# Attention into a squared-ReLU FFN on one core: the first batch planned, the second batch's q and k turned on TensorE

## The chip, the cores and the metric

The kernel runs on one core of one Trainium2 chip. The metric is the device time of one execution in microseconds (us). The program is one instruction stream for each of the five engines (TensorE, VectorE, ScalarE, GpSimd, SyncE), tied together by semaphores.

## What is computed

Grouped-query attention, whose output is reshaped to rows of tokens and goes straight into a feed-forward layer with a squared ReLU. Inputs and output are f32; the kernel computes in bf16 with f32 sums.

```python
batch, n_q_heads, n_kv_heads, seq, head_dim = (8, 16, 4, 384, 64)
k = np.repeat(k, group, axis=1); v = np.repeat(v, group, axis=1)   # group = 4
scores = np.matmul(q, k.transpose(0, 1, 3, 2)) / np.sqrt(D)
attn = softmax(scores)                       # max subtracted, rows divided by their sum
x = np.matmul(attn, v).transpose(0, 2, 1, 3).reshape(B * S, H * D)   # 3072 x 1024
h = np.maximum(x @ w_in, 0.0)                # 1024 -> 2048
out = (h * h) @ w_out                        # 2048 -> 1024
```

## The kernel before

**Recorder and planner.** Every operation goes through `Recorder.add`, which keeps for each engine a list in program order, works out the semaphore waits from the names of what is read and written, and advances a clock of its own per engine by a `cost` written by hand. Nothing is reordered at run time: the order in which operations were added is the order in which each engine carries them out. DMAs with the same `dma` tag also wait for one another. The estimated clocks are used by the main loop (L516 on) as a planner: at each step it lists what TensorE could do next (a value block `av`, a score burst `sc`, a piece of FFN `ffn`), estimates with `R.when` when the operands and a PSUM bank will be free, and takes by priority the first that is ready, or else the earliest.

**Attention of a batch.** There are four key groups of four query heads and 384 positions, that is 12 units of 128 keys. Keys are copied twice side by side in bf16 (`dup_k`, L241), so that two heads share TensorE as two halves of 64 rows. Keys and queries must then be transposed (`kT`, `qT`). Score bursts write PSUM; ScalarE applies the exponential into `expT` (L319, L339); a value block (`av`, L354) multiplies by the values, which carry a column of ones for the row sums; VectorE divides (L361, L367) into `o_sb`, which is transposed to `xT`, the FFN's input. `expT` holds 8 units, `o_sb` 3 groups, `xT` 3 batches; the staging tiles `q_st`, `k_st`, `v_st` hold 2 batches.

**Batch 0** is written out by hand ahead of the planner. Each key group gets a VectorE copy of its keys, transposes on TensorE (`turn_k_pe` L269, `turn_q_pe` L284) with evictions by VectorE (L274, L290), and then 18 small score bursts in all with exponentials of 128x1024 (L309, L319); value blocks and output turns on TensorE (L385, L391) are put in at fixed places. These turns use PSUM banks 6 and 7, the small bursts banks 0 to 5.

**Batches 1 to 7** are planned. GpSimd copies keys and values, and the DMA transposes of SyncE turn keys, both halves of the queries, and the outputs (`turn_k_dma` L250, `turn_q_dma` L256, `turn_o_dma` L372); all share the tag `turn`, so one runs at a time. Score bursts take two units at once over banks 0 to 5, with exponentials of 128x3072 (L329, L339).

**FFN.** For each batch, 16 column blocks of w_in in two half pieces each (L409), ReLU by VectorE (L419), square by ScalarE (L421), then 6 output blocks of w_out in four pieces each (L437), eviction (L449) and store (L452), on banks 6 and 7. It is the planner's lowest priority, and so fills TensorE wherever attention has nothing ready.

**Loads.** All loads are issued by GpSimd, which casts f32 to bf16 on the way, into one queue in program order: k, q and v of batch 0, four chunks of w_in, k, q and v of batch 1, four more chunks, and w_out in four parts. Loads of a later batch are issued when the staging tiles of two batches earlier are planned free. A warm-up of 24 matmuls on zeros (L486) precedes the work of TensorE.

Of the kernel before, what the change touches and what calls it, by code (L numbers as in the profile page):

```python
# [133 lines left out]
def bass_gqa_attention__then__ffn_squared_relu_kernel(  # L134
# [31 lines left out]
    q_st = [sb(f"q_st{i}", [128, H, NJ * D]) for i in range(NST)]  # L166
    k_st = [sb(f"k_st{i}", [128, NU, D]) for i in range(NST)]
    k_dup = [sb(f"k_dup{i}", [128, NU, 2, D]) for i in range(2)]
    v_st = [sb(f"v_st{i}", [128, NU, D]) for i in range(NST)]
# [28 lines left out]
    def load_k(b):  # L198
# [38 lines left out]
    def dup_k(b, eng, g0=0, g1=HKV):  # L237
        n = (g1 - g0) * NJ
        src = k_st[b % NST][:, g0 * NJ:g1 * NJ, :].unsqueeze(2).to_broadcast([128, n, 2, D])
        dst = k_dup[b % 2][:, g0 * NJ:g1 * NJ, :, :]  # L240
        R.add(eng, lambda e: e.tensor_copy(dst, src), reads=[("k_st", b % NST)],  # L241
              writes=[("k_dup", b % 2, g) for g in range(g0, g1)],
              cost=(0.15 * n / 3 + 0.1) if eng == "vector" else 0.33 * n)
# [17 lines left out]

    def turn_k_pe(b, g):
        i = pick((6, 7))
        pt = bank(i).bitcast(bf16)

        def tr(pe):
            for j in range(NJ):
                src = k_dup[b % 2][:, g * NJ + j].rearrange("p x d -> p (x d)")
                m = pe.matmul(pt[:, j * 128:(j + 1) * 128], src, ident[:], is_transpose=True)  # L269
# [7 lines left out]
    def turn_q_pe(b, g):  # L277
        i = pick((6, 7))
        pt = bank(i).bitcast(bf16)
# [22 lines left out]
    def burst_small(b, pieces, base):  # L302
# [3 lines left out]
        def sc(pe):  # L306
            for n, (u, c0) in enumerate(pieces):
# [11 lines left out]
        R.add("scalar", lambda e: e.activation(dst, src, AF.Exp, scale=0.125),  # L319
              reads=keys, writes=[("expT", (n + m) % NEX, c0 // 512) for m in range(len(pieces))], cost=0.89)  # L320

    def burst_two(b, u):

        def sc(pe):
            for k0, cols in ((0, ((0, 512), (512, 768))), (1, ((0, 256), (256, 768)))):
# [13 lines left out]
        R.add("scalar", lambda e: e.activation(dst, src, AF.Exp, scale=0.125),  # L339
              reads=keys, writes=[("expT", (n + m) % NEX, h) for m in range(2) for h in range(2)], cost=2.4)  # L340

# [36 lines left out]
    def turn_o_pe(b, c):  # L378
        i = pick((6, 7))
        pt = bank(i).bitcast(bf16)  # L380
# [95 lines left out]
    load_w_out(0, 0)  # L476
    load_w_out(0, 1)
    load_w_out(1, 0)
    load_w_out(1, 1)

# [3 lines left out]
    def warm_up(pe):  # L484
        for _ in range(24):
            m = pe.matmul(bank(7)[:, 0:256], warm[:, 0:128], warm[:, :])  # L486
        return m

    R.add("tensor", warm_up, reads=["warm"], writes=[("bank", 7)], cost=5.0)
# [7 lines left out]
    begun = -1  # L497
    todo = []
    for n, pieces in enumerate(smalls):
        g = pieces[-1][0] // NJ  # L500
        if g > begun:
            begun = g
            dup_k(0, "vector", g, g + 1)
            turn_k_pe(0, g)
            turn_q_pe(0, g)
            if g == 0:
                aug_v(0, "vector")
        burst_small(0, pieces, 2 * (n % 3))
        if n in (5, 8, 14):
            g = (5, 8, 14).index(n)  # L510
            todo += [lambda c=2 * g + i: av(0, c, (6, 7)) for i in range(2)]
            todo += [lambda c=2 * g + i: turn_o_pe(0, c) for i in range(2)]
        if todo:
            todo.pop(0)()
    while todo:
        todo.pop(0)()  # L516
# [4 lines left out]
    units, pairs, turned, x_done, up_done = NU, 6, 0, -1, -1  # L521
    loaded, queued = 1, 0
    chores = []
# [9 lines left out]
    def feed():  # L533
        for b in range(B):
            for n, item in enumerate(ffn(b)):
                yield (b, n) + item

    feeding = feed()
    f_head = next(feeding)
    margin = 0.5  # L540
    while av_q or sc_q or f_head is not None:
        now = R.clock["tensor"]
        if loaded + 1 < B and turned >= loaded + 1 - NST:
            loaded += 1
            load_k(loaded)
            load_q(loaded, 0, 16)
            load_v(loaded)
# [3 lines left out]
        while chores and R.when(reads=chores[0][0], eng="none") <= now + margin:  # L551
            chores.pop(0)[1]()
            if not chores:
                turned = queued
        cand = []
        if av_q:
            b, c = av_q[0]
            banks = (6, 7) if b == 0 else tuple(range(6))
            if units >= b * NU + (c // 2 + 1) * NJ and up_done >= b - NXT:
                t = max(R.when(reads=av_reads(b, c // 2)), min(R.when(writes=[("bank", i)]) for i in banks))  # L560
                cand.append((t, 0, "av"))
        if sc_q:
            b, u = sc_q[0]
            if turned >= b and pairs // 2 * NJ + NEX >= b * NU + u + 2:
                t = max(R.when(reads=score_reads(b, u) + score_reads(b, u + 1)),
                        R.when(writes=[("bank", i) for i in range(6)]))
                cand.append((t, 1, "sc"))
        if f_head is not None:
            b, n, need, banks, piece = f_head
            if x_done >= b:  # L570
                t = R.when(reads=need)
                if banks:
                    t = max(t, min(R.when(writes=[("bank", i)]) for i in banks))
                cand.append((t, 2, "ffn"))
        if not cand:
# [5 lines left out]
        what = min(ready, key=lambda x: x[1]) if ready else min(cand)  # L581
        if what[2] == "av":
            b, c = av_q.pop(0)
            av(b, c, banks=(6, 7) if b == 0 else tuple(range(6)))
            pairs += 1
            if b == 0:
                turn_o_pe(b, c)
            elif c % 2 == 1:
                turn_o_dma(b, c // 2)
            if c == 7:  # L590
                x_done = b
        elif what[2] == "sc":
            b, u = sc_q.pop(0)
            burst_two(b, u)
            units += 2
        else:
# [34 lines left out]
```

## Time and profile before

| | |
|---|---|
| runs | 460.81, 461.68, 464.22 us (median 461.68) |
| profiled execution | 463.22 us, with a span of 460.8 us from its first to its last instruction |
| TensorE busy | 431.8 us, 94% |
| mean granted TensorE clock | 0.963 |
| ScalarE, VectorE, GpSimd busy | 194.6, 157.7, 49.9 us |
| moved by DMA | 44.67 MB, mean 97 GB/s |

The profile is of one execution. PE is the matmul part of TensorE, PEld its weight loads, DVE is VectorE, ACT ScalarE, POOL GpSimd, SP SyncE; POOLq and SPq are the queues from which DMAs are issued. A line such as L329 is a line of the kernel; `ps<-qT,kT` names what an instruction writes and reads. A granted clock of 0.50 is half speed. Matmul durations are modelled to their end, so successive ones overlap; the distance between weight loads is nearer to the rate.

### The profile page before, as it was taken

The page shows a single profiled execution, that of the slowest core. Times are in us where ns is not written, and L with a number is a line of the kernel's source. Part 1 is how long each engine was busy: PE and PEld are TensorE (multiplying, and loading weights), DVE is VectorE, ACT ScalarE, POOL GpSimd, SP SyncE. Part 2 cuts the span into 40 slices and gives each one's busy share as a digit, 9 for nine tenths or more (in the row PEclk, how much of TensorE's full clock was granted, in tenths as well). Part 3 has the DMA queues.
Part 4 walks back from the last instruction along what each step waited for, and adds up shares of the span by engine and source line. Part 5 has one row for each costly group of instructions (what it writes and reads, how often), then busy time and mean ns, then how long its engine had stood idle before and what let it go on. Part 6 is the DMA issues. An engine that isn't in the chain of part 4 may idle for free.

```text
span 460.8 us, 7732 instructions
## 1 busy us (share of the span) xinstructions
PE 431.8 (94%) x3412; PEld 235.0 (51%) x3412; DVE 157.7 (34%) x328; ACT 194.6 (42%) x189; POOL 49.9 (11%) x59
## 2 busy tenths in 40 slices
PE   7668099997999999999999999999999999999997
PEld 4434055444565455554565554565465456445543
DVE  2343034222452244442344423353243224213411
ACT  3661067404766447744577445724033014103300
POOL 8740004013040200201000000000000000000000
PEclk9777589998999999999999999999999999999999
DMA  9999999769698796944705432004200110020011
GB/s 107 194 195 192 197 182 174 99 134 204 91 130 96 145 192 104 120 78 93 177 18 80 100 87 63 1 19 81 85 24 1 68 68 1 23 86 30 2 60 76
DMA packets 99762, 44.67 MB, mean 97 GB/s; under 512 B 81296, under 2 KB 93584, under 8 KB 99728
## 3 DMA queue, kind: packets, MB, share of 16 engines
q0 software_dynamic: 37488, 17.83, 31.6%
q1 hardware_dynamic: 62240, 26.35, 27.1%
q8 instruction: 26, 0.43, 0.4%
q14 instruction: 8, 0.07, 0.0%
HBM read 35.65 MB, written 12.58 MB: 105 GB/s over the span
## 4 chain that ended last, share of the span: by engine, by line
PE 90%; DMA 6%; ACT 2%; POOL 1%; DVE 1%; issue 0%
PE ps L437 36%; PE ps L409 36%; PE ps L354 8%; PE ps L329 7%; DMA qT<-q_st 3%; DMA kT<-k_dup 2%; ACT expT L319 1%; PE ps L486 1%; PE ps L309 1%; ACT expT L339 1%; POOL k_dup L241 0%; PE ps L385 0%; POOL q_st L214 0%; DVE qT L290 0%; POOL k_st L200 0%
## 5 line engine op out<-in xcount | busy, mean ns | idle before, releaser
L409 PE MATMUL ps<-xT,w_in_sb 128*128 128x384 bf16 x1024 | 177.2, 331 | 0.0
L437 PE MATMUL ps<-w_out_sb,h2T 128*128 128x512 bf16 x768 | 172.4, 379 | 0.0
L339 ACT ACTIVATE expT<-ps 128x3072 bf16<-128x3072 f32 x42 | 114.5, 2726 | 88.9 <-PE ps L329 88.2
L409 PEld LDWEIGHTS ps<-xT,w_in_sb 128*128 128x128 bf16 x1024 | 98.9, 99 | 72.5 <-issue 9.9
L421 ACT ACTIVATE h2T<-hr 128x384 bf16<-128x384 f32 x128 | 64.6, 520 | 139.7 <-DVE hr L419 139.6
L437 PEld LDWEIGHTS ps<-w_out_sb,h2T 128*128 128x128 bf16 x768 | 72.7, 98 | 87.8 <-issue 5.7
L419 DVE TENSOR_SCALAR hr<-ps 128x384 f32<-128x384 f32 x128 | 71.3, 557 | 122.2 <-PE ps L409 122.2
L449 DVE COPY y_sb<-ps 128x512 f32<-128x512 f32 x48 | 33.2, 692 | 125.1 <-PE ps L437 125.1
L354 PE MATMUL ps<-v_aug,expT 128*128 128x65 bf16 x1152 | 45.0, 199 | 7.6 <-ACT expT L319 4.7
L354 PEld LDWEIGHTS ps<-v_aug,expT 128*128 128x128 bf16 x1152 | 42.7, 101 | 15.3 <-ACT expT L319 5.5
L329 PE MATMUL ps<-qT,kT 64*128 64x512 bf16 (+1 forms) x336 | 35.2, 330 | 10.7 <-DMA qT<-q_st 10.7
L367 DVE TENSOR_TENSOR o_sb<-ps,rinv 128x384 bf16<-128x384 f32 x64 | 35.7, 558 | 2.2
L329 PEld LDWEIGHTS ps<-qT,kT 64*128 64x128 bf16 x336 | 13.1, 95 | 31.8 <-DMA qT<-q_st 11.1
L361 DVE RECIPROCAL rinv<-ps 128x6 f32<-128x6 f32 x64 | 12.2, 191 | 40.0 <-PE ps L354 39.9
L214 POOL DMA_DIRECT2D q_st<-in_q_dram x11 | 11.1, 1016 | 121.0 <-DMA qT<-q_st 121.0
L319 ACT ACTIVATE expT<-ps 128x1024 bf16<-128x1024 f32 x18 | 17.5, 1028 | 14.1 <-PE ps L309 14.1
L246 POOL COPY v_aug<-v_st 128x768 bf16<-128x768 bf16 x7 | 5.8, 831 | 64.8 <-PE ps L354 63.3
L309 PE MATMUL ps<-qT,kT 64*128 64x512 bf16 (+1 forms) x48 | 7.6, 387 | 3.3 <-DVE qT L290 2.6
L241 POOL COPY k_dup<-k_st 128x1536 bf16<-128x1536 bf16 x7 | 10.4, 1480 | 0.0
L224 POOL DMA_DIRECT2D w_in_sb<-in_moe_w_in_dram x8 | 7.1, 957 | 0.0
L200 POOL DMA_DIRECT2D k_st<-in_k_dram x8 | 6.2, 770 | 6.9 <-DVE k_dup L241 6.1
L486 PE MATMUL ps<-warm 128*128 128x256 bf16 x24 | 5.3, 416 | 1.1 <-DVE v_aug L482 1.1
(24 smaller groups left out, 37.8 us busy)
## 6 DMA issues: line engine op xcount, KB each, us to landing
out_dram<-y_sb SPq DMA_DIRECT2D x48, 256.0 KB, 2.0
q_st<-in_q_dram POOLq DMA_DIRECT2D x7, 768.0 KB, 11.5
w_in_sb<-in_moe_w_in_dram POOLq DMA_DIRECT2D x8, 512.0 KB, 17.0
w_out_sb<-in_moe_w_out_dram POOLq DMA_DIRECT2D x4, 1024.0 KB, 40.6
k_st<-in_k_dram POOLq DMA_DIRECT2D x8, 192.0 KB, 9.6
v_st<-in_v_dram POOLq DMA_DIRECT2D x8, 192.0 KB, 11.8
q_st<-in_q_dram POOLq DMA_DIRECT2D x4, 192.0 KB, 5.6
xT<-o_sb SPq DMA_TRANSPOSE x28, 2.9
```

What stands on the lines that cost most here:

```text
L309: m = pe.matmul(ps[:, base + x, n * wide:(n + 1) * wide], kT[b % 2][64 * x:64 * x + 64, u, :], q_cols(b, u // NJ, x, c0, c0 + wide))
L319: R.add("scalar", lambda e: e.activation(dst, src, AF.Exp, scale=0.125), reads=keys, writes=[("expT", (n + m) % NEX, c0 // 512) for m in r ...
L329: m = pe.matmul(flat[:, k0 * HC + c0:k0 * HC + c1], kT[b % 2][64 * x:64 * x + 64, u + k0, :], q_cols(b, (u + k0) // NJ, x, c0, c1))
L339: R.add("scalar", lambda e: e.activation(dst, src, AF.Exp, scale=0.125), reads=keys, writes=[("expT", (n + m) % NEX, h) for m in range(2) ...
L354: m = pe.matmul(po[:, f - 6 * s2, 0:D + 1], w, v_aug[b % 2][:, g * NJ + j, 0:D + 1], start=(j == 0), stop=(j == NJ - 1))
L361: R.add("vector", lambda e: e.reciprocal(rinv[r].ap().unsqueeze(2), po[:, :, D:D + 1]), reads=[("bank", i)], writes=[("rinv", r)], cost=0.13)
L367: R.add("vector", lambda e: e.tensor_tensor(dst, srcv, rbv, ALU.mult), reads=[("bank", i), ("rinv", r)], writes=[("o_sb", o, s2)], cost=0.48)
L409: m = pe.matmul(bank(i)[:, 0:S], w_in_sb[:, kc, c * 128:(c + 1) * 128], xT[b % NXT][:, kc, :], start=(kc == 0), stop=(kc == NKC - 1))
L419: R.add("vector", lambda e: e.tensor_scalar_max(hr[r][:, :], bank(i)[:, 0:S], 0.0), reads=[("bank", i)], writes=[("hr", r)], cost=0.48)
L421: R.add("scalar", lambda e: e.activation(h2T[b % 2][:, c, :], hr[r][:, :], AF.Square), reads=[("hr", r)], writes=[("h2T", b % 2, c)], cost ...
L437: m = pe.matmul(bank(i), h2T[b % 2][:, c, i3 * 128:(i3 + 1) * 128], w_out_sb[:, c, jj * 512:(jj + 1) * 512], start=(c == 0), stop=(c == NF ...
L449: R.add("vector", lambda e: e.tensor_copy(ysl, bank(i)), reads=[("bank", i)], writes=[("y", yb)], cost=0.61)
```

## The change

- **First loads.** Key group 0, then groups 1 to 3 of batch 0, go by SyncE's queue as f32 into a new tile `k_f32`, and the first four query heads by ScalarE's queue into `q_f32`; VectorE casts the latter into `q_st`. `dup_k` for batch 0 casts from `k_f32`: group 0 on VectorE, 1 to 3 on GpSimd, which also copies batch 0's values. The other queries and the values stay on GpSimd's queue.
- **Order on GpSimd's queue.** Three chunks of w_in instead of four precede batch 1, whose queries come in two halves; batch 1's key and value copies stand ahead of the four parts of w_out, and batch 0's copies ahead of the first chunk. Later batches' queries also come in two halves.
- **Batch 0 is planned**, with the same small bursts. The planner's candidates now are scores of batch 0 (priority 0), turns (1), value blocks (2), output turns on TensorE (3), scores of later batches (4), FFN (5). While batch 0 has scores left, turns and value blocks use banks 6 and 7, then banks 0 to 5.
- **Batch 1's keys and queries** are turned on TensorE, like batch 0's; a burst of batch 1 needs only its own group turned. From batch 2 on DMA transposes do it as before.
- **Tags.** `turn` becomes `turn_k`, `turn_q0`, `turn_q1` and `turn_o0` to `turn_o2`: different transposes don't wait for one another.
- **Costs.** The planner's cost of a small exponential goes from 0.89 to 0.92, of a large one from 2.4 to 2.63, of transposes from 3.0 to 2.0 (K) and 2.5 (Q).
- The warm-up has 14 matmuls instead of 24. In FFN 0 the first halves of the first two blocks come ahead of their second halves, and may start when four of the eight output turns are done and batch 0 has no scores left.

The core of the diff:

```diff
+    def first_loads():
+        for g0, g1 in ((0, 1), (1, HKV)):
+            R.add("sync", lambda e, g0=g0, g1=g1: e.dma_start(
+                k_f32[:, g0 * NJ:g1 * NJ, :].rearrange("p (g j) d -> p g (j d)", j=NJ),
+                k[0, g0:g1].rearrange("g (p j) d -> p g (j d)", j=NJ)),
+                writes=[("k_f32", g) for g in range(g0, g1)], dma=f"kf{g0}", cost=0.4 * (g1 - g0), issue=0.3)
+        R.add("scalar", lambda e: e.dma_start(
+            q_f32[:, :, :], q[0, 0:4].rearrange("h (p j) d -> p h (j d)", j=NJ)),
+            writes=["q_f32"], dma="qf", cost=1.3, issue=0.3)
...
-        src = k_st[b % NST][:, g0 * NJ:g1 * NJ, :].unsqueeze(2).to_broadcast([128, n, 2, D])
+        src = (k_st[b % NST] if b else k_f32)[:, g0 * NJ:g1 * NJ, :].unsqueeze(2).to_broadcast([128, n, 2, D])
...
-            writes=[("kT", b % 2, g) for g in range(HKV)], dma="turn", cost=3.0)
+            writes=[("kT", b % 2, g) for g in range(HKV)], dma="turn_k", cost=2.0)
...
-            writes=[("qT", b % 2, 2 * half + i) for i in range(2)], dma="turn", cost=3.0)
+            writes=[("qT", b % 2, 2 * half + i) for i in range(2)], dma=f"turn_q{half}", cost=2.5)
...
-            dma="turn", cost=2.0)
+            dma=f"turn_o{o}", cost=2.0)
...
-    load_k(0)
-    load_q(0, 0, 4)
+    first_loads()
+    load_q(0, 4, 8)
...
-    for h in (4, 8, 12):
-        load_q(0, h, h + 4)
-    for i in range(4):
+    load_q(0, 8, 12)
+    load_q(0, 12, 16)
+    for g in range(1, HKV):
+        dup_k(0, "gpsimd", g, g + 1)
+    aug_v(0, "gpsimd")
+    for i in range(3):
         load_w_in(i)
     load_k(1)
-    load_q(1, 0, 16)
+    load_q(1, 0, 8)
+    load_q(1, 8, 16)
     load_v(1)
-    for i in range(4, 8):
+    for i in range(3, 8):
         load_w_in(i)
+    dup_k(1, "gpsimd")
+    aug_v(1, "gpsimd")
...
-        for _ in range(24):
+        for _ in range(14):
...
+    dup_k(0, "vector", 0, 1)
+    R.add("vector", lambda e: e.tensor_copy(q_st[0][:, 0:4, :], q_f32[:, :, :]),
+          reads=["q_f32"], writes=[("q_st", 0, 0)], cost=0.5)
...
-    av_q = [(0, 6), (0, 7)] + [(b, c) for b in range(1, B) for c in range(8)]
-    sc_q = [(b, u) for b in range(1, B) for u in range(0, NU, 2)]
+    turn_q = [(b, g, w) for b in range(2) for g in range(HKV) for w in "kq"]
+    sc_q = [(0, n) for n in range(len(smalls))] + [(b, u) for b in range(1, B) for u in range(0, NU, 2)]
+    av_q = [(b, c) for b in range(B) for c in range(8)]
...
+            if b == 0:
+                items[1], items[2] = items[2], items[1]
...
+        first = bool(sc_q) and sc_q[0][0] == 0
+        spare = HIGH if first else LOW
-        if loaded + 1 < B and turned >= loaded + 1 - NST:
+        if loaded + 1 < B and turned >= loaded + 1 - NST and not turn_q:
...
+        if turn_q:
+            b, g, w = turn_q[0]
+            src = [("k_dup", b, g)] if w == "k" else [("q_st", b, g)]
+            cand.append((max(R.when(reads=src), open_bank(spare)), 1, "turn"))
...
+        if o_q:
+            cand.append((max(R.when(reads=o_q[0][2]), open_bank(spare)), 3, "o"))
...
-            if x_done >= b:
+            if x_done[b] >= 8 or (x_done[b] >= 4 and not first and b == 0 and n < 2):
```

More of the change, by code (lines that the diff above doesn't have):

```diff
@@ L167, in bass_gqa_attention__then__ffn_squared_relu_kernel @@
     k_st = [sb(f"k_st{i}", [128, NU, D]) for i in range(NST)]
+    k_f32 = sb("k_f32", [128, NU, D], f32)
+    q_f32 = sb("q_f32", [128, 4, NJ * D], f32)
     k_dup = [sb(f"k_dup{i}", [128, NU, 2, D]) for i in range(2)]
@@ L238, in dup_k @@
         n = (g1 - g0) * NJ
-        src = k_st[b % NST][:, g0 * NJ:g1 * NJ, :].unsqueeze(2).to_broadcast([128, n, 2, D])
+        src = (k_st[b % NST] if b else k_f32)[:, g0 * NJ:g1 * NJ, :].unsqueeze(2).to_broadcast([128, n, 2, D])
         dst = k_dup[b % 2][:, g0 * NJ:g1 * NJ, :, :]
-        R.add(eng, lambda e: e.tensor_copy(dst, src), reads=[("k_st", b % NST)],
+        R.add(eng, lambda e: e.tensor_copy(dst, src), reads=[("k_st", b % NST)] if b else [("k_f32", g) for g in range(g0, g1)],
               writes=[("k_dup", b % 2, g) for g in range(g0, g1)],
@@ L275, in turn_k_pe, with turn_q_pe @@
               reads=[("bank", i)], writes=[("kT", b % 2, g)], cost=0.27)
-    def turn_q_pe(b, g):
-        i = pick((6, 7))
+    def turn_q_pe(b, g, banks):
+        i = pick(banks)
         pt = bank(i).bitcast(bf16)
@@ L319, in burst_small @@
         R.add("scalar", lambda e: e.activation(dst, src, AF.Exp, scale=0.125),
-              reads=keys, writes=[("expT", (n + m) % NEX, c0 // 512) for m in range(len(pieces))], cost=0.89)
+              reads=keys, writes=[("expT", (n + m) % NEX, c0 // 512) for m in range(len(pieces))], cost=0.92)
     def burst_two(b, u):
@@ L339, in burst_two @@
         R.add("scalar", lambda e: e.activation(dst, src, AF.Exp, scale=0.125),
-              reads=keys, writes=[("expT", (n + m) % NEX, h) for m in range(2) for h in range(2)], cost=2.4)
+              reads=keys, writes=[("expT", (n + m) % NEX, h) for m in range(2) for h in range(2)], cost=2.63)
     def av_reads(b, g):
@@ L466, in bass_gqa_attention__then__ffn_squared_relu_kernel @@
     load_v(0)
-    for h in (4, 8, 12):
-        load_q(0, h, h + 4)
-    for i in range(4):
+    load_q(0, 8, 12)
[4 more added lines that the diff above has]
+    for i in range(3):
         load_w_in(i)
     load_k(1)
-    load_q(1, 0, 16)
+    load_q(1, 0, 8)
+    load_q(1, 8, 16)
     load_v(1)
-    for i in range(4, 8):
+    for i in range(3, 8):
         load_w_in(i)
[L476 to L479, printed above, removed]
+    dup_k(1, "gpsimd")
+    aug_v(1, "gpsimd")
+    for jj in range(2):
+        for part in range(2):
+            load_w_out(jj, part)
     for i in range(2):
@@ L484, in warm_up @@
     def warm_up(pe):
-        for _ in range(24):
+        for _ in range(14):
             m = pe.matmul(bank(7)[:, 0:256], warm[:, 0:128], warm[:, :])
         return m
-    R.add("tensor", warm_up, reads=["warm"], writes=[("bank", 7)], cost=5.0)
+    R.add("tensor", warm_up, reads=["warm"], writes=[("bank", 7)], cost=2.9)
+    dup_k(0, "vector", 0, 1)
+    R.add("vector", lambda e: e.tensor_copy(q_st[0][:, 0:4, :], q_f32[:, :, :]),
+          reads=["q_f32"], writes=[("q_st", 0, 0)], cost=0.5)
+    ALL, LOW, HIGH = tuple(range(8)), tuple(range(6)), (6, 7)
     smalls = []
@@ L496, in bass_gqa_attention__then__ffn_squared_relu_kernel @@
             smalls.append([(u - 1, 512), (u, 512)])
[L497 to L516, printed above, removed]
-    av_q = [(0, 6), (0, 7)] + [(b, c) for b in range(1, B) for c in range(8)]
-    sc_q = [(b, u) for b in range(1, B) for u in range(0, NU, 2)]
-    units, pairs, turned, x_done, up_done = NU, 6, 0, -1, -1
-    loaded, queued = 1, 0
+    turn_q = [(b, g, w) for b in range(2) for g in range(HKV) for w in "kq"]
+    sc_q = [(0, n) for n in range(len(smalls))] + [(b, u) for b in range(1, B) for u in range(0, NU, 2)]
+    av_q = [(b, c) for b in range(B) for c in range(8)]
+    o_q = []
+    turned_g = set()
+    units, halves, pairs, turned, up_done = 0, set(), 0, 1, -1
+    x_done = {b: 0 for b in range(B)}
+    loaded, queued = 1, 1
     chores = []
@@ L534, in feed, with open_bank @@
         for b in range(B):
-            for n, item in enumerate(ffn(b)):
+            items = list(ffn(b))
+            if b == 0:
+                items[1], items[2] = items[2], items[1]
+            for n, item in enumerate(items):
                 yield (b, n) + item
+    def open_bank(banks):
+        return min(R.when(writes=[("bank", i)]) for i in banks)
     feeding = feed()
@@ L581, in bass_gqa_attention__then__ffn_squared_relu_kernel @@
         what = min(ready, key=lambda x: x[1]) if ready else min(cand)
-        if what[2] == "av":
+        if what[2] == "turn":
+            b, g, w = turn_q.pop(0)
+            (turn_k_pe if w == "k" else turn_q_pe)(b, g, spare)
+            turned_g.add((w, b, g))
+        elif what[2] == "av":
             b, c = av_q.pop(0)
-            av(b, c, banks=(6, 7) if b == 0 else tuple(range(6)))
+            av(b, c, spare)
             pairs += 1
             if b == 0:
-                turn_o_pe(b, c)
+                o_q.append((b, c, [("o_sb", (b * HKV + c // 2) % 3, c % 2)]))
             elif c % 2 == 1:
                 turn_o_dma(b, c // 2)
-            if c == 7:
-                x_done = b
+                x_done[b] += 2
+        elif what[2] == "o":
+            b, c, _ = o_q.pop(0)
+            turn_o_pe(b, c, spare)
+            x_done[b] += 1
         elif what[2] == "sc":
             b, u = sc_q.pop(0)
-            burst_two(b, u)
-            units += 2
+            if b == 0:
+                burst_small(0, smalls[u], 2 * (u % 3))
+                halves |= {(p[0], p[1] // 512) for p in smalls[u]}
+                while (units, 0) in halves and (units, 1) in halves:
+                    units += 1
+            else:
+                burst_two(b, u)
+                units += 2
         else:
```

36 lines of the change are left out of this document (22 added, 14 removed).

## The prediction

> **What bounds the kernel now.** I read the page first, then the waits of TensorE, then the stretches of five microseconds, then the chain. Page, parts 1 and 2:
>
> ```profile
> span 460.8 us, 7732 instructions
> PE 431.8 (94%) x3412; PEld 235.0 (51%) x3412; DVE 157.7 (34%) x328; ACT 194.6 (42%) x189; POOL 49.9 (11%) x59
> PE   7668099997999999999999999999999999999997
> PEclk9777589998999999999999999999999999999999
> DMA  9999999769698796944705432004200110020011
> ```
>
> A slice is 11.5 us. TensorE is full from the sixth slice to the end, with one dent in the tenth; all its idle time, 460.8 - 431.8 = 29.0 us, lies in the first five slices, in that dent and at the two ends, and in the same places the granted clock is low. So what can be won is in the first 65 us, and whatever happens later is worth something only if TensorE runs dry again. Who it waits for there (view of waits; the columns are total, times, longest):
>
> ```profile
> PE ps L329 <- DMA qT<-q_st: 10.7, 1, 10.7
> PE ps L354 <- ACT expT L319: 4.7, 3, 2.2
> PE ps L354 <- ACT expT L339: 2.8, 1, 2.8
> ...
> ACT expT L319 <- PE ps L309: 14.1, 9, 6.3
> ```
>
> One wait of 10.7 us is the first score burst of batch 1, which needs qT from a DMA transpose. The last row is ScalarE in batch 0: 14.1 us without scores, 6.3 of them before its first exponential. The view of stretches, with busy time and count per engine, then the granted clock:
>
> ```profile
> 20.00:25.00 5.00, 4.61 (x52) 2.80 (x52) 2.16 (x7) 3.10 (x4) 0.00 (x0) 0.66 1.54 194
> ...
> 35.00:40.00 5.00, 3.34 (x29) 2.39 (x30) 2.15 (x6) 0.00 (x0) 0.00 (x0) 0.50 1.35 181
> 40.00:45.00 5.00, 5.00 (x28) 2.86 (x27) 1.67 (x3) 1.55 (x3) 0.00 (x0) 0.88 1.30 203
> 45.00:50.00 5.00, 0.82 (x6) 0.29 (x3) 0.56 (x1) 0.54 (x2) 0.00 (x0) 0.80 1.22 193
> 50.00:55.00 5.00, 0.00 (x0) 0.00 (x0) 0.00 (x0) 0.00 (x0) 0.00 (x0) 0.50 1.22 196
> 55.00:60.00 5.00, 3.45 (x15) 1.47 (x16) 0.56 (x1) 1.95 (x1) 0.00 (x0) 0.50 1.25 206
> 60.00:65.00 5.00, 5.00 (x30) 2.45 (x28) 1.12 (x2) 2.90 (x5) 0.00 (x0) 0.83 1.22 197
> ...
> 110.00:115.00 5.00, 5.00 (x52) 3.15 (x50) 2.06 (x5) 1.10 (x2) 0.00 (x0) 0.71 1.41 248
> ```
>
> While TensorE stands still the DMA engines move 193 to 206 GB/s: the weights. The transposes run among them, as the chain shows (start, length):
>
> ```profile
> 30.14 11.34 DMA kT<-k_dup
> 41.49 15.01 DMA qT<-q_st
> ...
> 457.67 0.69 DVE y_sb L449
> ```
>
> and page part 6, with the medians over all batches from issue to landing in the last column:
>
> ```profile
> out_dram<-y_sb SPq DMA_DIRECT2D x48, 256.0 KB, 2.0
> ...
> q_st<-in_q_dram POOLq DMA_DIRECT2D x4, 192.0 KB, 5.6
> ...
> qT<-q_st SPq DMA_TRANSPOSE x14, 3.7
> kT<-k_dup SPq DMA_TRANSPOSE x7, 3.6
> ```
>
> A transpose that takes 3.6 us elsewhere took 11.3 and 15.0 us beside the weights. That is the stall.
>
> **The change part by part.** The sum is made against the profiled execution: 463.22 us, 2.4 us of it outside its span of 460.8. The runs shown have a median of 461.68, so 1.5 us come off at the end. The rows for batch 0, from the timeline (start, length):
>
> ```profile
> 5.94 0.47 PEld L269 LDWEIGHTS ps<-ident,k_dup 128*128 128x128 bf16 x3
> ...
> 8.35 5.61 ACT L319 ACTIVATE expT<-ps 128x1024 bf16<-128x1024 f32 x6 [6.33 <-PE ps L309]
> 8.86 0.68 DVE L246 COPY v_aug<-v_st 128x768 bf16<-128x768 bf16 x1 [1.00 <-DMA v_st<-in_v_dram]
> ...
> 9.85 0.17 PEld L269 LDWEIGHTS ps<-ident,k_dup 128*128 128x128 bf16 x3 [0.33 <-DVE k_dup L241]
> ...
> 9.97 0.38 PEld L284 LDWEIGHTS ps<-ident,q_st 128*128 128x128 bf16 x6
> ...
> 28.62 1.48 POOL L241 COPY k_dup<-k_st 128x1536 bf16<-128x1536 bf16 x1
> ...
> 31.67 2.00 ACT L319 ACTIVATE expT<-ps 128x1024 bf16<-128x1024 f32 x2 [0.18 <-PE ps L309]
> ...
> 36.07 1.20 PE L354 MATMUL ps<-v_aug,expT 128*128 128x65 bf16 x18
> ...
> 38.34 0.26 PEld L409 LDWEIGHTS ps<-xT,w_in_sb 128*128 128x128 bf16 x2
> ```
>
> and from the page, part 5:
>
> ```profile
> L319 ACT ACTIVATE expT<-ps 128x1024 bf16<-128x1024 f32 x18 | 17.5, 1028 | 14.1 <-PE ps L309 14.1
> ...
> L486 PE MATMUL ps<-warm 128*128 128x256 bf16 x24 | 5.3, 416 | 1.1 <-DVE v_aug L482 1.1
> ```
>
> 1. The start. Warm-up goes from 24 to 14 matmuls: 1.1 + 5.3 x 14/24 = 4.2 us instead of 6.4. The first keys (96 KB in f32) and the first four heads (384 KB) now come by the queues of SyncE and ScalarE. The trace has no such load: the nearest rows are 2.0 us for 256 KB out on SyncE's queue and 5.6 for 192 KB on GpSimd's. Issued at about 1.2, they are there between 3.2 and 6.8; I take the hardware row, 3.5. VectorE then casts q (no such row; 0.68, from the 768-column copy): 4.2, level with the end of warm-up. From the first key transpose at 5.94 to the first exponential at 8.35 it took 2.4, so the first exponential comes at 6.6: -1.7 (0 to -2.2).
>
> 2. Batch 0's exponentials. Eighteen of them are 17.5 us busy, but run from 8.35 to 33.67, 25.3: 7.8 us of holes, because each new key group sits in program order behind a VectorE copy, two transposes and two evictions, while values and their evictions fill the queue. The planner now issues scores first and turns the groups ahead of need. The six at 8.35 show 0.93 each with nothing between. Bounds 0 to -7.8; I take -6.0, leaving 0.6 for each of three groups.
>
> 3. The end of batch 0. From the last exponential (33.67) to the first FFN weights (38.34) pass 4.7 us at a granted clock of 0.50, for two value blocks and four turns that need about 1.9 at full clock. Now batch 1's turns and scores can stand between: -2.8 (0 to -4.7).
>
> 4. The 10.7 us wait: batch 1's K and Q no longer go through the DMA transposes. -10.7. What is late next is the arrival of q of batch 1 itself, still on GpSimd's queue behind three weight chunks; by the planner's costs its second half lands at 27.3, about when batch 0 ends, so there I put no more than the allowance in step 8.
>
> 5. The clock after that wait: 5.00 x 0.12 + 3.45 x 0.50 + 5.00 x 0.17 = 3.2 us in the stretches from 40 to 65. With no standstill ahead of them: -3.2 (0 to -3.2). The Trainium skill, page TensorE: Matmul & The Clock Gate, section Part 1, says that the clock halves after an idle window of about 3.4 us and comes back after as much sustained work; by that rule this term goes entirely, and the trace agrees (0.50 after the 10.7 us).
>
> 6. The dent near 107: 2.8 us waiting for an exponential, and 5.00 x 0.29 = 1.5 at the lower clock after it. It arose where the planner had no FFN piece ready, with every transpose chained behind one tag; the tags are now split and the exponential's cost is nearer the truth. It may come back elsewhere: -2.5 (0 to -4.3).
>
> 7. Batch 1's turns on TensorE: four groups of 0.17 + 0.38 = 0.55 by the weight loads at full clock: +2.2 (0 where they fall into holes of batch 0, 3.4 at the clock of the first group). Their eight evictions on VectorE lie beside FFN work, where it is under half busy.
>
> 8. What may be late instead. GpSimd now makes three key copies of batch 0 (a quarter of 1.48 each, more from f32) and the values' copy ahead of the first weights, and batch 1's copies ahead of w_out. The queue behind has a backlog, so w_out should come no later than now; batch 1's attention outputs still turn by DMA among the weights, and hold o_sb, thus VectorE. The nearest rows are 3.7 unloaded and 15.0 loaded, so 0 to +11; as FFN work is ready behind, I take the lower side: +1.0. The Trainium skill, page SBUF — State Buffer, section SBUF: two separate sides, says that GpSimd and a VectorE copy in a two-port mode exclude each other for a whole instruction, and that an f32 copy keeps GpSimd from writing descriptors: by it the start would lose up to another microsecond. No row here shows that case.
>
> Sum: -1.7 - 6.0 - 2.8 - 10.7 - 3.2 - 2.5 + 2.2 + 1.0 = -23.7; 463.2 - 23.7 = 439.5, and 1.5 off gives **438**. All terms at their better ends (-32.9) give 429.
>
> **The rivals.** Within 1% (457.1 to 466.3) a measurement could hardly tell from no change.
>
> *B, batch 0 is no shorter.* TensorE's order was dense before too: 4.61 of 5.00 busy at 20 to 25, at a clock of 0.66. If the clock stays low, the turns, scores and values of batch 0 take as long as ScalarE's exponentials, and terms 2 and 3 vanish: 438 + 8.8 = 446.8. For it: the clock row reads 7 in slices two and three already, where TensorE is 6 tenths busy. Against it: the exponential holes were waits on order, which the new order removes. The clock page's rule (above) would give this outcome only if the holes stay.
>
> *C, the wait moves to batch 2.* Its K and Q are still turned by DMA, now just behind w_out. The planner allows 0.1 + 0.8 + 2.5 + 1.2 = 4.6 us for half of Q; if it takes the loaded 15.0, TensorE, which follows a fixed order, stands 10.4 us, and loses 1.8 at low clock: 438 - 1.0 + 12.2 = 449.2. For it: 11.3 and 15.0 above. Against it: the weights have landed by then, and batch 1 still owes its FFN.
>
> *B and C together*: 449.2 + 8.8 = 458.0, no change that can be told.
>
> *D, slower: the transposes without their common chain.* Until now one tag let one transpose run at a time. Now those of K, of both halves of Q and of the outputs are in flight together and share the engines; the planner counts each as if alone. It decides from (461.7 - 438)/6 = 4.0 us of lateness in each of batches 2 to 7; at 5 each the time is 438 + 30 = 468. For it: loaded transposes are three to four times as long. So is the DMA row, at 4 to 9 tenths up to 230 us. Against it: with the chain, TensorE had no such wait there, and the transposes wait for their inputs at different times.
>
> **How the numbers follow.** My sum 0.60 (431 to 445), B 0.20, C 0.10, B with C 0.05, D 0.05. Faster by over 1%: 0.60 + 0.20 + 0.10 = 0.90; within 1%: 0.05; slower: 0.05. The range goes from 429, all terms at their better ends, to 451, so that B and C are inside; 0.10 lie above it.
>
> **What would show it.** Right: the first exponential near 6.6; the last of batch 0's eighteen near 25; no wait of L329-type scores on qT in batch 1; first FFN matmuls near 28; TensorE full at clock 1.00 from there, idle time about 15 us in all. Wrong: slices two and three still at 6 and clock 0.7 (B); a wait of some 10 us on qT between 60 and 90 (C); waits on qT or xT in every batch after 100 (D); VectorE standing at o_sb (L367), which would make term 8 too small.

## The result, and the profile after

The changed kernel takes 444.38 us (median of 4 runs, 443.82 to 444.94), the kernel before 462.95 (4 runs, 460.81 to 465.73): a ratio of 0.9596, interval 0.9536 to 0.9655. (The median of 461.68 above is that of three of these four runs.) Beside another experiment (run e10), with 6 runs, the changed kernel took 444.75 us, a ratio of 0.9572 (0.9528 to 0.9617). The forecast was 438, in a range of 429 to 451. The profiled execution took 443.82 us, with a span of 442.0, 18.8 less than before.

The page, parts 1 and 2:

```profile
span 442.0 us, 7776 instructions
PE 423.0 (96%) x3438; PEld 230.2 (52%) x3438; DVE 159.0 (36%) x333; ACT 193.1 (44%) x189; POOL 55.1 (12%) x68
PE   7799999199999999999999999999999999999997
PEclk9999999699999999999999999999999999999999
```

A slice is 11.05 us. Where the kernel before had five slices of holes and low clock, there are two of moderate holes at full clock, and then one new hole, the eighth slice, where TensorE is one tenth busy. TensorE's waits:

```profile
PE ps L342 <- DMA qT<-q_st: 9.7, 1, 9.7
PE ps L322 <- ACT expT L332: 2.4, 5, 0.5
```

That is the same kind of wait as before, 9.7 us now instead of 10.7, on a different line number only because the file grew: a first score burst waits for qT. It is batch 2's. The stretches around it (busy per engine, granted clock):

```profile
75.00:80.00 5.00, 2.15 (x10) 0.78 (x8) 0.69 (x1) 0.00 (x0) 0.28 (x1) 1.00 1.39 178
80.00:85.00 5.00, 0.00 (x0) 0.00 (x0) 0.00 (x0) 0.00 (x0) 0.00 (x0) 0.50 1.39 179
85.00:90.00 5.00, 3.10 (x13) 1.04 (x14) 0.00 (x0) 1.59 (x1) 2.18 (x3) 0.50 1.19 218
90.00:95.00 5.00, 5.00 (x33) 2.59 (x32) 1.62 (x3) 3.08 (x3) 3.25 (x4) 0.98 1.39 151
```

and the chain that ended last:

```profile
69.66 3.21 SPq L263
72.91 13.94 DMA qT<-q_st
86.90 1.46 PE ps L342 x8
```

Batch 0, in the timeline:

```profile
0.73 0.45 ACTq L214 DMA_DIRECT2D q_f<-in_q_dram  x1
...
4.73 0.90 DVE L509 CAST q_st<-q_f 128x768 bf16<-128x768 f32 x1 [0.62 <-DMA q_f<-in_q_dram]
...
7.28 16.61 ACT L332 ACTIVATE expT<-ps 128x1024 bf16<-128x1024 f32 x18 [4.79 <-PE ps L322]
...
26.44 0.33 PE L282 MATMUL ps<-ident,k_dup 128*128 128x128 bf16 x3
...
28.45 1.46 PE L422 MATMUL ps<-xT,w_in_sb 128*128 128x384 bf16 x8
...
30.24 0.82 PE L342 MATMUL ps<-qT,kT 64*128 64x512 bf16 x8 [0.32 <-DVE qT L303]
```

All eighteen exponentials run without a hole, from 7.28 to 23.89; before, the last ended at 33.67. Batch 1's first scores start at 30.24 instead of 56.55, 26.3 us earlier. Not all of that is lead: the kernel before had done 36 FFN matmuls by then, the changed one 16, and at 0.16 us each the difference is some 3 us by estimate. The change ends 18.8 us ahead. So part of the lead is given back at batch 2, and more than the difference shows, since the dent near 107 is gone too.

### The profile page after: what moved, and what is told of

The parts are those of the page before. It is cut to its first block, busy times and chain, and to the rows that moved or that the text cites. A ratio compares the mean times of both kernels' runs of the same rounds, so it can differ in the third digit from the quotient of the medians.

```text
span 442.0 us, 7776 instructions
## 1 busy us (share of the span) xinstructions
PE 423.0 (96%) x3438; PEld 230.2 (52%) x3438; DVE 159.0 (36%) x333; ACT 193.1 (44%) x189; POOL 55.1 (12%) x68
## 4 chain that ended last, share of the span: by engine, by line
PE 89%; DMA 4%; ACT 3%; DVE 2%; SPq 1%; issue 0%
PE ps L422 38%; PE ps L450 36%; PE ps L367 7%; PE ps L342 7%; DMA qT<-q_st 3%; ACT expT L332 3%; DMA q_f<-in_q_dram 1%; SPq L263 1%; DVE qT L303 1%; DVE y_sb L462 0%; DVE o_sb L380 0%; DVE kT L287 0%; DVE xT L404 0%; DVE q_st L509 0%; PE ps L322 0%
## 5 line engine op out<-in xcount | busy, mean ns | idle before, releaser
L422 PE MATMUL ps<-xT,w_in_sb 128*128 128x384 bf16 x1024 | 174.1, 326 | 0.0
L422 PEld LDWEIGHTS ps<-xT,w_in_sb 128*128 128x128 bf16 x1024 | 97.1, 98 | 69.2 <-issue 5.6
L342 PE MATMUL ps<-qT,kT 64*128 64x512 bf16 (+1 forms) x336 | 35.2, 330 | 10.1 <-DMA qT<-q_st 9.7
L367 PEld LDWEIGHTS ps<-v_aug,expT 128*128 128x128 bf16 x1152 | 39.8, 97 | 6.1 <-DVE rinv L374 0.5
L367 PE MATMUL ps<-v_aug,expT 128*128 128x65 bf16 x1152 | 41.3, 193 | 0.0
L227 POOL DMA_DIRECT2D q_st<-in_q_dram x17 | 14.9, 886 | 44.1 <-DMA qT<-q_st 43.4
L259 POOL COPY v_aug<-v_st 128x768 bf16<-128x768 bf16 x8 | 6.7, 832 | 98.2 <-PE ps L367 87.6
L332 ACT ACTIVATE expT<-ps 128x1024 bf16<-128x1024 f32 x18 | 16.6, 1112 | 4.8 <-PE ps L322 4.8
L322 PE MATMUL ps<-qT,kT 64*128 64x512 bf16 (+1 forms) x48 | 6.7, 329 | 3.2 <-ACT expT L332 2.4
L220 POOL DMA_DIRECT2D v_st<-in_v_dram x8 | 6.3, 784 | 0.1
```

Source lines behind the costliest of these rows:

```text
L227: R.add("gpsimd", lambda g: g.dma_start(q_st[st][:, h0:h1, :], q[b, h0:h1].rearrange("h (p j) d -> p h (j d)", j=NJ)), writes=[("q_st", st ...
L342: m = pe.matmul(flat[:, k0 * HC + c0:k0 * HC + c1], kT[b % 2][64 * x:64 * x + 64, u + k0, :], q_cols(b, (u + k0) // NJ, x, c0, c1))
L367: m = pe.matmul(po[:, f - 6 * s2, 0:D + 1], w, v_aug[b % 2][:, g * NJ + j, 0:D + 1], start=(j == 0), stop=(j == NJ - 1))
L422: m = pe.matmul(bank(i)[:, 0:S], w_in_sb[:, kc, c * 128:(c + 1) * 128], xT[b % NXT][:, kc, :], start=(kc == 0), stop=(kc == NKC - 1))
```

## The experiments

Three questions: why batch 2's transposes are late, why that costs time although FFN work is ready, and what each part of the change is worth. Each kernel is an edit of the changed one unless said otherwise; ratios are to the kernel before.

**e5: batch 3's loads later.** In the changed kernel the loads of batches 2 and 3 are planned one right after the other as soon as batch 1's turns are, so batch 3's run where batch 2's transposes run. Here batch 3's wait for batch 2's turns to be planned. Only GpSimd's order changes; the orders of TensorE, VectorE, ScalarE and SyncE are the same as in the changed kernel.

```diff
-        if loaded + 1 < B and turned >= loaded + 1 - NST and not turn_q:
+        if loaded + 1 < B and turned >= loaded + 1 - NST + (loaded == 2) and not turn_q:
```

> Batch 3's loads are issued only when batch 2's turns have been planned; TensorE's, VectorE's, ScalarE's and SyncE's orders stay as they are. Theory that the loads of batch 3 slow batch 2's transposes: kT and the halves of qT land in 3 to 6 us each, the wait at batch 2 falls from 9.7 to 3 us or less, and the time to about 436. Theory that the transposes slow one another: the wait stays at 8 to 10 us, the time at 444.

Measured: 433.18 us, 0.9413 (0.9375 to 0.9452). The transposes of batch 2 from issue to landing, changed kernel first, then this one (view of DMA, issues between 70 and 73, and between 69.6 and 73):

```profile
kT<-k_dup SPq DMA_TRANSPOSE x1, 10.8
qT<-q_st SPq DMA_TRANSPOSE x1, 13.9
```

```profile
kT<-k_dup SPq DMA_TRANSPOSE x1, 6.6
qT<-q_st SPq DMA_TRANSPOSE x1, 5.7
```

and TensorE's wait for them:

```profile
PE ps L342 <- DMA qT<-q_st: 0.6, 1, 0.6
```

This is the first theory's outcome, with a time 3 us below its 436: the loads made the transposes late. They are not the only weight on them: K at 6.6 is still above the 3.6 of the median. In the changed kernel the last load of batch 3 was issued at 36.55 (first row, POOL) and landed 48.7 later (second row), at 85.25; the first half of Q landed at 86.85.

```profile
36.55 0.84 POOL L220 DMA_DIRECT2D v_st<-in_v_dram  x1
```

```profile
v_st<-in_v_dram POOLq DMA_DIRECT2D x1, 192.0 KB, 48.7
```

**e2: one tag again.** All transposes share the tag `turn`, so they run one at a time.

```diff
-dma="turn_k", cost=2.0)
+dma="turn", cost=2.0)
...
-dma=f"turn_q{half}", cost=2.5)
+dma="turn", cost=2.5)
...
-dma=f"turn_o{o}", cost=2.0)
+dma="turn", cost=2.0)
```

> All DMA transposes share one tag again, so that one runs at a time and the planner counts them so. Theory that they slow one another when in flight together: each lands in 4 to 6 us, the first half of Q earlier than 86.9, the wait falls to 4 us or less, the time to about 438. Theory that batch 3's loads slow them: each still takes about 10, they come one after the other, the wait stays at 8 us or grows, the time is 443 to 450.

Measured: 441.90 us, 0.9604 (0.9556 to 0.9652), with a wait of 7.2 us:

```profile
PE ps L342 <- DMA qT<-q_st: 7.2, 1, 7.2
```

SyncE's queue in this kernel:

```profile
69.85 1.21 SPq L385 DMA_TRANSPOSE xT<-o_sb  x1
...
77.37 1.50 SPq L263 DMA_TRANSPOSE kT<-k_dup  x1
83.49 5.12 SPq L269 DMA_TRANSPOSE qT<-q_st  x2
```

Neither expectation came out whole. Single transposes are shorter (K 6.1, the first half of Q 3.7), but K now waits for the last output of batch 1 to land and starts at 77.37 instead of 69.66. By then most of batch 3's loads are through (the last one, issued at 36.60, lands 43.9 later, at 80.5), so the shorter times don't show that transposes slow one another; that part stays open. What the run does show is that the wait stands with one tag too, so the split tags did not make it; at most they made it 2.5 us longer.

**e3: the planner told the truth.** Nothing changes but three cost figures of batch 2.

```diff
-dma="turn_k", cost=2.0)
+dma="turn_k", cost=8.7 if b == 2 else 2.0)
...
-dma=f"turn_q{half}", cost=2.5)
+dma=f"turn_q{half}", cost=(7.7, 1.5)[half] if b == 2 else 2.5)
```

> Only the planner's costs of batch 2's three transposes are changed, to what the profile of the changed kernel shows (landed at 80.5, 86.9 and 88.4). Theory that the wait is a matter of TensorE's fixed order, with FFN 1 ready all the time: FFN pieces come ahead of the first scores of batch 2, the wait falls under 2 us, nothing is added: 444.4 - 9.7 - 1.8 = 433. Rival (there is not enough ready work, or the later attention is missed further on): a wait of 4 us or more remains somewhere, 438 to 444.

Measured: 432.55 us, 0.9401 (0.9362 to 0.9440), as the theory had it. The transposes are as slow as ever (view of DMA, issues between 69.6 and 73):

```profile
kT<-k_dup SPq DMA_TRANSPOSE x1, 10.8
qT<-q_st SPq DMA_TRANSPOSE x1, 14.8
```

but TensorE doesn't meet them, because 64 FFN matmuls stand ahead of the first scores:

```profile
73.80 4.70 PE L450 MATMUL ps<-w_out_sb,h2T 128*128 128x512 bf16 x21
78.33 10.56 PE L422 MATMUL ps<-xT,w_in_sb 128*128 128x384 bf16 x64
88.83 0.82 PE L342 MATMUL ps<-qT,kT 64*128 64x512 bf16 x8
```

The work to fill the hole had been there all the time. The wait needs both links: e5 removes the late transpose, e3 the order that counted on an early one, and either is enough to end it.

**e1: batch 2 on TensorE too.** `turn_q` runs over three batches; batch 2 gets its key and value copies but no DMA transposes; loads of batch 4 and later wait until its turns are planned.

```diff
-    turn_q = [(b, g, w) for b in range(2) for g in range(HKV) for w in "kq"]
+    turn_q = [(b, g, w) for b in range(3) for g in range(HKV) for w in "kq"]
...
-        if turn_q:
+        if turn_q and (turn_q[0][0] < 2 or turned >= 2):
...
-                ok = (("q", b, (u + 1) // NJ) in turned_g) if b == 1 else turned >= b
+                ok = (("q", b, (u + 1) // NJ) in turned_g) if b < 3 else turned >= b
```

> Batch 2's keys and queries are turned on TensorE too, as batch 1's are. Theory (the 9.7 us wait of the changed kernel is the DMA transposes of batch 2, nothing else): the wait goes, with the 1.8 us at half clock behind it, and four groups of turns cost 2.2 us: 444.4 - 9.7 - 1.8 + 2.2 = 435. Rival (the wait belongs to whichever batch is first to go by DMA, since batch 3's transposes run among the loads of batch 4): a wait of some 5 to 10 us appears at batch 3, and the time is 441 to 446.

Measured: 435.41 us, 0.9459 (0.9418 to 0.9499), the theory's outcome; no wait for qT at any batch. The rival had one part right: batch 3's transposes, the first by DMA here, are as slow as batch 2's were (view of DMA, issues between 77 and 81).

```profile
kT<-k_dup SPq DMA_TRANSPOSE x1, 11.3
qT<-q_st SPq DMA_TRANSPOSE x1, 15.6
```

But TensorE has other work in front of their scores, so this lateness costs nothing. The time is 2.9 us above e3. The turns of batch 2 take TensorE about 2.0 us of it (70.93 to 72.94 in the timeline), near the 2.2 that I had; the rest I have not traced.

**e7 and e11: batch 1 on TensorE and nothing else.** On the kernel before: batch 1's key and value copies and its turns come after the hand-written batch 0, and its DMA transposes go. e11 is the same file beside the changed kernel on one chip.

```diff
...
     while todo:
         todo.pop(0)()
+    dup_k(1, "gpsimd")
+    aug_v(1, "gpsimd")
+    for g in range(HKV):
+        turn_k_pe(1, g, tuple(range(6)))
+        turn_q_pe(1, g, tuple(range(6)))
...
-    units, pairs, turned, x_done, up_done = NU, 6, 0, -1, -1
-    loaded, queued = 1, 0
+    units, pairs, turned, x_done, up_done = NU, 6, 1, -1, -1
+    loaded, queued = 1, 1
```

> The kernel before with batch 1's keys and queries turned on TensorE, and nothing else of the change. Theory: the 10.7 us wait at batch 1 and 3.2 us of low clock go, 2.2 to 3.4 us of turns come, and TensorE comes to batch 2 late enough to find its transposes done: 461.6 - 10.7 - 3.2 + 2.5 = 450. Rival (the wait moves to batch 2, as it did in the changed kernel): 455 to 460.

> Batch 1 alone on TensorE in the kernel before, on the same chip as the changed kernel: theory that the rest of the change brings nothing as long as the wait at batch 2 is there: within 2.5 us of the changed kernel, 444 to 446.5. Rival (its 446.0 came from another chip): 449 or more.

Measured: 446.02 us, 0.9594 (0.9533 to 0.9655), and in e11 444.87 us, 0.9593 (0.9549 to 0.9638), beside 444.75 for the changed kernel. One part of the change is worth as much as the whole of it. In e7 the wait at batch 1 is gone and none comes at batch 2, as the theory had it; the time is 4 us below its 450, and the dent near 107, which it had left in, is gone as well. Batch 1's first scores start at 41.00, 10.8 us later than in the changed kernel:

```profile
41.00 0.82 PE L329 MATMUL ps<-qT,kT 64*128 64x512 bf16 x8
```

Yet TensorE waits for no transpose; its longest wait is one for an exponential of batch 0:

```profile
PE ps L354 <- ACT expT L319: 4.1, 2, 2.3
PE ps L309 <- DVE qT L290: 2.6, 4, 0.7
```

Batch 2's transposes were issued from 77.87 (K) and 84.33 (Q) on, when the last load of batch 3 had landed (38.70 + 38.0 = 76.7), and K took no longer than the median (issues between 77 and 79):

```profile
kT<-k_dup SPq DMA_TRANSPOSE x1, 3.6
```

**e4: all but batch 1's turns.** The changed kernel with batch 1's keys and queries turned by DMA: the planned batch 0 and the f32 loads alone.

```diff
-    turn_q = [(b, g, w) for b in range(2) for g in range(HKV) for w in "kq"]
+    turn_q = [(b, g, w) for b in range(1) for g in range(HKV) for w in "kq"]
...
-    units, halves, pairs, turned, up_done = 0, set(), 0, 1, -1
+    units, halves, pairs, turned, up_done = 0, set(), 0, 0, -1
...
-    loaded, queued = 1, 1
+    loaded, queued = 1, 0
...
```

> The changed kernel with batch 1's keys and queries turned by DMA again: the planned batch 0 and the f32 loads alone. Theory (batch 0 ends ten microseconds earlier, but TensorE then stands longer at batch 1's transposes, which run among the weights whatever TensorE does): a wait of 14 us or more at batch 1 instead of 10.7, none at batch 2, 453 to 460 in all. Rival (the two parts add up): the wait at batch 1 is 10.7 as before and the time 444.4 + 10.7 + 3.2 - 2.2 - 11.5 = 445.

Measured: 449.64 us, 0.9671 (0.9619 to 0.9722): between the two expectations, and neither. TensorE waits twice, 7.1 us at batch 1 (to 40.63) and 7.5 at batch 2:

```profile
PE ps L342 <- DMA qT<-q_st: 14.6, 2, 7.5
```

I had left out that batch 1's key copy is ready sooner, so its transposes start at 22.66 instead of 30.14. They take no less (15.2 for the issue after 33), but end at 40.6 instead of 56.5. The wait at batch 2 I had thought gone with the later arrival of TensorE; but the loads are later too: batch 3's last one is issued at 48.72 instead of 36.55, because its staging tiles wait for batch 1's slow transposes.

**e6: first loads as before**, on e3, where no later wait can swallow a difference: keys and the first heads by GpSimd's cast.

```diff
...
-    first_loads()
+    load_k(0)
+    load_q(0, 0, 4)
     load_q(0, 4, 8)
...
-    R.add("vector", lambda e: e.tensor_copy(q_st[0][:, 0:4, :], q_f32[:, :, :]),
-          reads=["q_f32"], writes=[("q_st", 0, 0)], cost=0.5)
```

> On the kernel with the true costs of batch 2's transposes (432.6): the first keys and heads by GpSimd's cast again, all else planned. Theory (the start counts in full, since nothing hides it): the first exponential moves from 7.3 to 8.3 or later, and GpSimd's two more loads put batch 0's copies 1.5 us back: 434 to 435. Rival (the start is hidden behind the loads of the weights): 432.6.

Measured: 434.57 us, 0.9341 (0.9291 to 0.9390), with the first exponential at 8.48:

```profile
8.48 16.63 ACT L332 ACTIVATE expT<-ps 128x1024 bf16<-128x1024 f32 x18 [6.46 <-PE ps L322]
```

e8, on the same chip, has the f32 loads and otherwise nearly the same program, and took 433.00, with the first exponential at 7.79. Of the 1.6 us between them, 0.7 are there at the first exponential; e6's profile also has a granted clock of 0.74 from 20 to 25, where e8's has 1.00, and the runs of the two overlap (433.13 to 435.23 and 431.88 to 434.01). What the f32 loads are worth is therefore open.

**e8: the old costs of the exponentials**, on e3.

```diff
-cost=0.92)
+cost=0.89)
...
-cost=2.63)
+cost=2.4)
```

> On the kernel with the true costs of batch 2's transposes (432.6): the planner's costs of the exponentials put back to 0.89 and 2.4. Theory that these costs made the dent near 107 in the kernel before: a wait of some 2.8 us of value blocks on an exponential comes back, with its low clock: 435 to 437. Rival (the chained tag or the place in the order made it): no such wait, 432.6.

Measured: 433.00 us, 0.9310 (0.9261 to 0.9360), the rival's outcome: no wait of a value block on an exponential. e2 (old tag), e8 (old costs) and e7 (both) are all without the dent near 107, so neither the tag nor the costs made it. Its cause is open; it was seen only in the kernel before, of which there is one profile.

**e9: late loads and a cost of 4.5 for batch 2's first half of Q**, to remove e5's last 0.6 us.

```diff
-dma=f"turn_q{half}", cost=2.5)
+dma=f"turn_q{half}", cost=4.5 if b == 2 and half == 0 else 2.5)
```

> The changed kernel with batch 3's loads issued late and the planner's cost of batch 2's first half of Q raised from 2.5 to 4.5, to take away the last 0.6 us of waiting. Theory: 432 to 433, the time of the kernel with true costs (432.6), since what is left of TensorE's idle time lies in batch 0 and at the ends. Rival: the two edits together uncover another gain, under 431.

> The changed kernel itself beside the run above on the same chip: 444, and so 11 to 12 us above it.

Measured: 432.77 us, 0.9318 (0.9279 to 0.9356), and 444.75 for the changed kernel beside it, 12.0 us more. e3, e5, e8 and e9 all end at 432.6 to 433.2: whichever of these ways the wait is removed, the rest is the same. e3 needs nothing but three figures:

```profile
span 430.3 us, 7778 instructions
PE 421.3 (98%) x3438; PEld 229.8 (53%) x3438; DVE 158.8 (37%) x333; ACT 193.3 (45%) x189; POOL 55.3 (13%) x68
```

TensorE is idle for 9.0 us in it, about 4 of them at the two ends.

## Why the prediction was right, and where its steps were not

The time lies inside the range and the sign was right, but 444.4 is not the 438 of the likeliest case. What happened was that case's gains, some of them larger than forecast, and on top of them rival C, which had been given 0.10. That 444.4 even lies in the band of my own sum (431 to 445) is luck: in the spans, steps 2 and 6 and a remainder brought 6.6 us more than forecast, and the other steps 11.5 us less, 10.4 of them at batch 2. Step by step, in the profiled executions:

1. *The start.* The first exponential came at 7.28, not 6.6: -1.1 instead of -1.7, inside the bounds. In the profiles of other runs with the same loads it came between 6.91 (e3) and 7.80 (e9), so a step of this size is not settled by one. The load by ScalarE's queue took 3.97 us from issue to landing, against 2.0 for the store row that I had gone by, and the f32 cast 0.90 instead of 0.68.
2. *Batch 0's exponentials.* From first to last 16.6 instead of 25.3 us: -8.7, beyond the bound of -7.8, because the eighteen without holes are also shorter in sum (16.6 against 17.5). I kept 0.6 for each group as unavoidable; the planner's early turns hid it all.
3. and 7. *The end of batch 0, and batch 1's turns.* From the last exponential to steady FFN work 23.89 to 28.45, 4.6 us against 4.7 before: the turns, from 26.44 on, fill the time saved. Together -0.1; I had -2.8 + 2.2 = -0.6. The trace of the kernel before has two output turns there (35.77 and 38.15), not the four that I had read.
4. *The wait at batch 1* is gone, but for 0.3 us behind the last evictions: -10.7, as said. My remark that batch 1's data arrive as batch 0 ends held.
5. *The clock.* Full from 0 to 80, so the 3.2 us did go. But 3.10 x 0.50 + 5.00 x 0.02 = 1.7 came back behind the new wait; in sum -1.5. Of the 3.2, the first 0.6 (40 to 45) lay ahead of the wait, not behind it.
6. *The dent:* gone, -4.3 instead of -2.5. My reason for it (tag and cost) fell with e2, e7 and e8.
8. *What may be late instead.* I put +1.0 on bounds of 0 to +11. It was 9.7. This is the step that failed, and it was mis-sized for a wrong reason: "as FFN work is ready behind, I take the lower side". Ready work helps only if the order has it there. The planner had put batch 2's scores at the point where its own estimate said that they were ready, and TensorE carries them out in that order; e3 shows that the ready FFN work would have covered the delay in full. What was late was not what the step looks at (w_out and batch 1's outputs), but batch 2's K and Q, which it had left to rival C.

The sum of these is -1.1 - 8.7 - 0.1 - 10.7 - 1.5 - 4.3 + 9.7 = -16.7 against a difference of 18.8 in the spans. Two things that no step had account for the remaining 2.1, by estimate. The changed kernel does 8 FFN matmuls of batch 0 ahead of its last exponentials (first two rows below), 8 x 0.16 = 1.3 us. The kernel before began its FFN at half clock (third row; the granted clock was 0.50 from 35 to 40): from 38.44 to 40 that cost 1.56 x 0.50 = 0.8 us, which lies between step 3 and step 5.

```profile
21.52 0.82 PE L422 MATMUL ps<-xT,w_in_sb 128*128 128x384 bf16 x4
...
23.29 0.81 PE L422 MATMUL ps<-xT,w_in_sb 128*128 128x384 bf16 x4
```

```profile
38.44 6.73 PE L409 MATMUL ps<-xT,w_in_sb 128*128 128x384 bf16 x32
```

*Rival C* had the place, the mechanism and the size (10.4 us and 1.8 at low clock, for 9.7 and 1.7). The arguments against it were that the weights have landed by then and that batch 1 still owes its FFN. The second is answered under step 8. The weights had landed, at about 64.1, but I looked at the weights alone. The change also lets the loads of batches 2 and 3 follow one another at once, since turning batch 1 on TensorE frees its staging tiles early: these loads were the traffic, and e5 shows it. Its time, 449.2, was too long only because the other terms were better. I had read the diff's new condition on loading (`and not turn_q`) as a delay and not asked which loads it releases together.

*Rival B* did not occur: batch 0 became shorter, and in the profiled execution its clock stayed at 1.00 throughout. (In e10's, the same kernel, it was 0.66 from 20 to 25, and the eighteen exponentials still ran without a hole.) On the new wait, the trace agrees with the Trainium skill's rule of the clock (page TensorE: Matmul & The Clock Gate, section Part 1): 0.50 after 9.7 us of idling, and 0.98 in the stretch from 90.

*Rival D* did not occur: after batch 2 TensorE waits for no transpose.

By the Trainium skill, page SBUF — State Buffer, section SBUF: two separate sides, the start would have lost up to a microsecond by the estimate in step 8. No such loss shows: GpSimd issued two loads at 0.75 each (first row below), and its own key copies began at 5.55, after waiting for the keys alone. But only the second of these issues overlapped the f32 cast at 4.73, and only in part, so the run is no full test.

```profile
3.76 1.50 POOL L227 DMA_DIRECT2D q_st<-in_q_dram  x2
...
5.55 1.41 POOL L254 CAST k_dup<-k_f 128x384 bf16<-128x384 f32 x3 [0.30 <-DMA k_f<-in_k_dram]
```

The parts, each to the kernel before:

| | batch 1 by DMA | batch 1 on TensorE |
|---|---|---|
| batch 0 by hand | 1 | 0.9594 (e7), 0.9593 (e11) |
| batch 0 planned, f32 loads | 0.9671 (e4) | 0.9596, 0.9572 (e10) |
| the same, no wait at batch 2 | not tried | 0.9401 (e3), 0.9310 (e8), 0.9318 (e9) |

The kernel before, to which these ratios are, had medians from 461.6 to 465.5, so what two rows differ by is better read from runs made side by side: 446.02 (e7) and 433.00 (e8), and 444.87 (e11), 432.77 (e9) and 444.75 (e10). Beside the turns on TensorE, all the rest of the change is worth nothing as long as batch 2 waits, and 12 to 13 us once it does not. What TensorE wins early it loses again at the next thing that comes by DMA at its own pace.

## What to carry to other kernels

When a change brings the bounding engine forward, list what comes next by DMA and when it lands: the DMA timetable moves with the engine only where a load waits for it, and the loads that the change lets go earlier are in it. With a fixed order, work that is ready covers a delay only where the planner knows of the delay; a planner's cost for a transfer has to be the cost beside the traffic at that place, and correcting three such figures was worth 12 us here. Where one part of a change gives the whole gain, look for the wait that swallowed the others.

## What the runs showed of the hardware

- A DMA transpose of 12 tiles took 3.6 us from issue to landing where the DMA engines had a share of 0.43 (e7, 77 to 82), 5.7 to 7.8 between the loads of one batch and those of the next (e5), and 9.6 to 15.6 beside continuous loads (the changed kernel and e1), at shares of 1.3 to 1.4 in the changed kernel.
- SyncE itself can be held while it issues, and whatever is behind, stores here, waits. Beside loads, the two query transposes held its queue for 5.75 and 5.82 us in the changed kernel (the row below has both), and for 4.61 and 4.01 in the kernel before, where one runs at a time; in e2, issued when the loads had landed, for 1.41 and 1.44.

```profile
72.91 11.62 SPq L269 DMA_TRANSPOSE qT<-q_st  x2
```

- The busy share of a stretch alone does not tell the granted clock. From 20 to 25 the changed kernel had 1.00 in one execution and 0.66 in another (e10), with TensorE 4.20 and 4.21 of 5 us busy.

```profile
20.00:25.00 5.00, 4.20 (x84) 3.06 (x85) 1.66 (x6) 3.89 (x5) 1.47 (x1) 1.00 1.60 191
```

```profile
20.00:25.00 5.00, 4.21 (x48) 2.87 (x49) 0.75 (x2) 3.88 (x5) 1.47 (x1) 0.66 1.60 191
```
